# A new order at both ends of a fused attention and gated-convolution kernel, and a broadcast split over two DMA queues

## The chip, the cores and the metric

The kernel runs on one core of one Trainium2 chip. The metric is the device time of one execution in microseconds, and the comparison is between the median before the change and the median after it. The three runs of the kernel before took 1071.4, 1070.09 and 1071.84 us.

## The reference

Four independent batches. `q` has 12288 rows of 128 numbers per batch, `kv` is an image of 384 x 32 positions of 128 channels.

```python
kv_pool = kv.reshape(B, H // 4, 4, W // 4, 4, C).mean(axis=(2, 4))
k = v = kv_pool.reshape(B, -1, C) @ w_sr            # 768 keys per batch
s = (q @ k.T) / sqrt(C)
a = exp(s - s.max(-1)); a /= a.sum(-1) + 1e-9
x = a @ v                                            # attention output
gate_pre[t] = sum over k in 0..4 of conv_w[k] * x[t + k - 4]   # causal, zeros before the start
out = (sigmoid(gate_pre) * (x @ w_val)) @ w_out
```

The kernel works on transposed arrays, with the 128 channels as partitions and the rows of `q` along the free dimension.

## The kernel before

**Groups and tiles.** The rows of `q` are cut into 96 groups of 512 (24 for each batch), and a group into 4 tiles of 128 rows, `j` = 0 to 3. The main loop has one step for each tile, 384 in all. The order of the instructions on every engine is the order in which the Python code emits them (a manual schedule); each engine and each DMA queue works through its own list in that order. In the step of tile `j` of group `cur`, earlier groups are at later stages: `last` is one group behind, `avg` two, `xg` three, `mg` four, `og` five.

**One tile.** TensorE computes the scores (`score`, L264: each factor is split in a high and a low part, so three matmuls for each half of the 768 keys). VectorE takes the row maximum (`row_max`, L269, tile `nm`). ScalarE computes the exponentials and their sums (`expo`, L281). ScalarE writes the high part of the exponentials in 16 bits (`p_hi`, L328) and VectorE the low part (`p_lo`, L332, one step later). The exponentials must be transposed before the product with the values. This is done in one of two ways. For tiles `j < by_dma`, high and low parts go to `hl`, and SyncE's queue (SP) issues a DMA transpose from `hl` to `pt` (L336), one for tiles 0 and 1 and one for the rest. For the other tiles (`on_pe`) the exponentials go to `pf`, TensorE transposes them (`turn`, L311), and the parts are written straight to `pt`. Then TensorE multiplies with the values in 18 matmuls for each group (`av_range`, L345).

**The normaliser.** The four columns of sums of a group lie in `z`. When the group is complete, VectorE takes the reciprocal (L288) and transposes it to `r` (L293). `norm_store` (L299) writes the 512 numbers to a DRAM tile `rd` in four small DMAs, and `norm_rows` (L304) reads them back as one row that is broadcast to 128 partitions, into `rb`. In the loop both are on SP's queue: `norm_store(last)` at `j` = 1, `norm_rows(last)` at `j` = 3. `g_x` (L362) multiplies the product with `rb` and gives `x` of the group, one group after `norm_rows` was emitted.

**After x.** POOL computes the products of the convolution's taps (L372, the last tap on ScalarE, L370) and adds them (L381). ScalarE takes a tanh (`th`, L407), TensorE the value projection (`g_val`, L411), VectorE the gate (`g_h`, L416), TensorE the output projection (`g_out`, L421), ScalarE the scaled copy to `o` (`g_evac`, L431), and SP stores two groups together (L435). `new_x` copies the last 4 columns of the previous group's `x` ahead of the new one (L358). PSUM has three two-bank tiles for the scores (`bank_pair`, pool `ps_s`), one bank for `av` and one for all small products (`misc`, tile `m`).

**The start.** The first batch's `kv` comes in 16 pieces (tiles `kvt`, 384 KB each). Pieces 0, 2, 4 and 6 are pooled on POOL (L133), the others on VectorE (L121). When pieces 0 to 7 are pooled, and again after piece 13 and after piece 15, TensorE projects the finished keys (L146, tile `m`), ScalarE writes their high part (`kh`, L153) and the values (`vt`, L154), and VectorE the low part (`kl`, L157). The scores of the first three tiles follow: the first halves after the first projection, the second halves after the last.

**The end.** After the loop stands code written out by hand for the last five groups, `n1` (the last) to `n5`: the product of `n2`, the normaliser of `n1` (its `rd` and `rb` on ScalarE's queue), the product of `n1` in two halves of 256 rows (`avs`), then the convolutions of `n2` and `n1`, which `conv_mixed` splits between ScalarE (products in `kvt` tiles, L389) and VectorE (`fast`, L395, L397 and L401), and the projections and stores (L439).

Of the kernel before, what the change touches and what calls it, by code (L numbers as in the profile page):

```python
# [16 lines left out]
P = 128  # L17
GQ = 512
BLOCK = 32
NT = GQ // P  # L20


# [5 lines left out]
def attn_moe_kernel(ctx, tc, qT, kvT, w_sr, w_moe, outT):  # L28
# [34 lines left out]
    def misc():  # L63
        return ps_m.tile([P, GQ], F32, name="m")
# [185 lines left out]
    def bank_pair():  # L250
        return ps_s.tile([P, 2, GQ], F32, name="s")
# [42 lines left out]

    def norm_store(g, eng):

        g.rd = dram.tile([NT, P], F32, name="rd")
        for i in range(0, P, BLOCK):
            eng.dma_start(out=g.rd[:, i:i + BLOCK], in_=g.r[i:i + NT])  # L299

    def norm_rows(g, eng):
        g.rb = work.tile([C, GQ], F32, name="rb", bufs=3)
        row = g.rd.rearrange("(o j) p -> o (j p)", o=1)
        eng.dma_start(out=g.rb, in_=row.broadcast_to([C, GQ]))  # L304

    def turn(g, j):

# [3 lines left out]
            nc.tensor.transpose(g.s[j][:, k // (NCH // 2), c:c + P], pf[:, k * P:(k + 1) * P],  # L311
                                ident)

    def pt_tile(g):
        if g.pt is None:
            g.pt = ptp.tile([P, NT, 2 * NCH, P], F16, name="pt")
        return g.pt

    def part(g, j, a):

        if on_pe(g, j):
            return pt_tile(g)[:, j, a * NCH:(a + 1) * NCH].rearrange("p (h k) q -> p h (k q)", h=2)
# [7 lines left out]
    def p_lo(g, j):  # L330

        nc.vector.scalar_tensor_tensor(out=part(g, j, 1), in0=g.s.pop(j), scalar=2.0 ** 15,  # L332
                                       in1=part(g, j, 0), op0=ALU.mult, op1=ALU.subtract)
        if (j % 2 or j == g.by_dma - 1) and not on_pe(g, j):
            j0 = j // 2 * 2
            nc.sync.dma_start_transpose(  # L336
                out=pt_tile(g)[:, j0:j + 1].rearrange("p j k q -> p (j k) q"),
                in_=g.hl[:, j0:j + 1].rearrange("p j a k -> p (j a k)"))

    AV_ORDER = [(v, k, a) for k in range(NCH) for v, a in (("vh", 0), ("vl", 0), ("vh", 1))]  # L340
# [1 line left out]
    def av_range(g, out, lo, hi, j0=0, j1=NT):  # L342
        for i in range(lo, hi):
            v, k, a = AV_ORDER[i]
            nc.tensor.matmul(out, g.st[v][:, k * P:(k + 1) * P], g.pt[:, j0:j1, a * NCH + k],  # L345
                             start=(i == 0), stop=(i == len(AV_ORDER) - 1))

    def av_part(g, part):
# [94 lines left out]
    for b in range(B):  # L443
        for i in range(NG):
            g = Group()
            g.i, g.b, g.t0, g.st = len(groups), b, i * GQ, states[b]
            g.by_dma = 4 if i % 2 == 0 and (b == B - 1 or not 0 < i <= PIECES + 1) else 3
            g.s, g.nm, g.pf, g.hl, g.pt = {}, {}, {}, None, None
            groups.append(g)
    G = len(groups)  # L450

    def at(i):
# [17 lines left out]
    for i in range(1, PIECES + 1):  # L470
        if i - 1 + AHEAD < PIECES:
            load_kv(0, st, i - 1 + AHEAD)
        (pool_halving if i - 1 in by_pool else pool_kv)(st, i - 1)
        if low and i - 1 in ends:
            low()
        if i == PIECES // 2:
            g_qh(at(0))
            g_ql(at(0))
        if i in ends:
            project(st, ends[i], misc())  # L480
            high, low = split_keys(st, ends[i])
            high()
        if i == PIECES // 2 + 1:
            for j in first:
                score(at(0), j, (0,))
    low()
# [105 lines left out]
    gate2 = conv_mixed(n2, 0, GQ)  # L592
    n2.th = g_tanh(gate2)
    m2, o2 = pair_of(GQ)
    g_val(n2, m2)
    new_x(n1, n2, nc.scalar.copy)
    g_x(n1, avs[0], *cuts[0])
    h4 = g_h(n4.th, n4.m)
    n4.m = g_out(h4, misc())
    out_tile(n4)  # L600
    gates = [conv_mixed(n1, *cuts[0])]
    g_evac(n4, n4.m)
    store(n4)
    g_x(n1, avs[1], *cuts[1])
    m3, o3 = pair_of(GQ)
    g_val(n3, m3)
    g_out(g_h(n2.th, m2), o2)
    n3.th = g_tanh(n3.gate)
    ms = pair_of(half)
    g_val(n1, ms[0], *cuts[0])  # L610
    gates.append(conv_mixed(n1, *cuts[1]))
    out_tile(n2)
    g_evac(n2, o2)
    store(n2)
    g_out(g_h(n3.th, m3), o3)
    g_val(n1, ms[1], *cuts[1])
    n1.th = work.tile([C, GQ], F32, name="th")
    ths = [g_tanh(gate, n1.th[:, c0:c1]) for gate, (c0, c1) in zip(gates, cuts)]
    g_evac(n3, o3)
    store(n3)  # L620
    for th, m, o, c in zip(ths, ms, pair_of(half), cuts):
        g_evac(n1, g_out(g_h(th, m), o), *c)
        store(n1, *c)


# [26 lines left out]
```

## Time and profile before

| what | us |
|---|---|
| median of 3 runs | 1071.4 (1070.09 to 1071.84) |
| the profiled execution's own time | 1068.99 |
| its span (first to last instruction of the core) | 1067.2 |
| TensorE matmul busy in the span | 1021.7 (96%) |
| VectorE, ScalarE, POOL busy | 918.1 (86%), 910.6 (85%), 874.5 (82%) |

The span is what the views of the profile show, from 0 to 1067.2 us; the execution's own time is 1.8 us longer. PE means TensorE's matmuls, PEld its weight loads, DVE VectorE, ACT ScalarE, SPq and ACTq the DMA-issuing instructions on SyncE's and ScalarE's queues. In a row of the timeline stand the start, the duration, the engine, the line, the operation, output and input, the count, and in brackets how long the engine stood idle before it and what ended that. A row of the chain (the work that ended last, followed back) has a start, a length and a piece of work. In a table by stretches stand, for each engine, the busy time and the count, then the granted clock of TensorE, the busy share of the 16 DMA engines, and GB/s.

### The profile page before, as it was taken

To read this page: it belongs to the slowest core of one execution; us is meant where nothing else is said; L and a number is where in the kernel's file an instruction comes from. 1 tells how busy PE (TensorE), PEld (TensorE's weight loads), DVE (VectorE), ACT (ScalarE), POOL (GpSimd) and SP (SyncE) were. 2 spreads that over 40 slices of the span, in tenths; PEclk is the share of its full clock that TensorE was granted. 3 is DMA by queue.
4 is the path that set the end of the run, shared out by engine and by line. 5 is a ranking of instruction groups with operands and counts; after the bars stand their busy time and mean duration, and the time that the engine had idled before them with its cause. 6 is when DMAs were issued, how large, how long until landed. Compare 5 with 4: busy or idle time off the path is not lost.

```text
span 1067.2 us, 16368 instructions
## 1 busy us (share of the span) xinstructions
PE 1021.7 (96%) x4912; PEld 686.6 (64%) x4912; DVE 918.1 (86%) x1283; ACT 910.6 (85%) x1671; POOL 874.5 (82%) x964
## 2 busy tenths in 40 slices
PE   2799999999999999999999999999999999999996
PEld 1666666666666666666666666666666666666663
DVE  6788899898888999999888999999888888888885
ACT  1788888888988888889888888888898898988883
POOL 4178888888888888888888888888888898988882
PEclk9999999999999999999999999999999999999999
DMA  8699999999999999999999999999999899989984
GB/s 288 120 219 218 221 216 241 216 201 208 199 209 231 218 242 223 223 216 212 195 199 231 238 225 217 245 213 200 196 210 207 198 208 215 207 192 200 211 178 123
DMA packets 526263, 224.96 MB, mean 211 GB/s; under 512 B 492640, under 2 KB 493024, under 8 KB 526176
## 3 DMA queue, kind: packets, MB, share of 16 engines
q1 hardware_dynamic: 526000, 223.66, 97.4%
q8 instruction: 39, 0.64, 0.2%
q14 instruction: 48, 0.39, 0.1%
q10 hardware_dynamic: 176, 0.26, 0.1%
HBM read 75.83 MB, written 25.36 MB: 95 GB/s over the span
## 4 chain that ended last, share of the span: by engine, by line
PE 74%; DVE 11%; ACT 9%; POOL 2%; issue 2%; DMA 2%; SPq 0%; DVEq 0%; ACTq 0%; POOLq 0%
PE s L264 30%; PE av L345 25%; PE m L411 7%; PE m L421 5%; PE s L311 4%; ACT s L281 4%; DVE nm L269 3%; ACT hl L328 2%; DVE h L416 2%; POOL ql L248 2%; DVE x L362 1%; DVE hl L332 1%; ACT qh L244 1%; DMA rb<-rd 1%; PE m L146 1%
## 5 line engine op out<-in xcount | busy, mean ns | idle before, releaser
L345 PE MATMUL av<-pt,vh 128*128 128x512 f16 x1140 | 386.9, 381 | 1.8 <-DVE x L362 1.4
L381 POOL TENSOR_TENSOR sum<-sum,tap 128x512 f32<-128x512 f32 x282 | 361.1, 1280 | 22.1
L269 DVE TENSOR_REDUCE nm<-s 128x1 f32<-128x768 f32 x384 | 361.4, 941 | 2.0 <-PE s L264 1.9
L281 ACT ACTIVATE s<-s,nm 128x768 f32<-128x768 f32 x312 | 272.5, 873 | 76.9 <-DVE nm L269 73.3
L372 POOL TENSOR_SCALAR tap<-x,wm 128x512 f32<-128x512 f32 x376 | 253.4, 693 | 80.0 <-DVE x L362 78.5
L332 DVE SCALAR_TENSOR_TENSOR hl<-s,hl 128x768 f16<-128x768 f32 x312 | 296.9, 952 | 23.8 <-ACT hl L328 23.6
L264 PE MATMUL s<-kh,qh 128*128 128x384 f32 x768 | 257.0, 415 | 8.1 <-DVE pw L174 2.1
L328 ACT ACTIVATE hl<-s 128x768 f16<-128x768 f32 x312 | 252.6, 810 | 9.1
L345 PEld LDWEIGHTS <-vh 128*128 128x128 f16 x1164 | 113.5, 97 | 178.4 <-issue 79.7
L345 PE MATMUL av<-pt,vl 128*128 128x512 f16 x570 | 216.0, 379 | 0.0
L264 PE MATMUL s<-kl,qh 128*128 128x384 f32 x768 | 198.8, 339 | 0.3 <-DVE kl L157 0.3
L264 PE MATMUL s<-kh,ql 128*128 128x384 f32 x768 | 198.8, 339 | 0.0
L264 PEld LDWEIGHTS s<-kh,qh 128*128 128x128 f32 x768 | 137.8, 191 | 65.8 <-issue 29.1
L248 POOL TENSOR_TENSOR ql<-q,qh 128x512 fp32r<-128x512 f32 x96 | 122.1, 1272 | 66.1 <-ACT qh L244 65.6
L264 PEld LDWEIGHTS s<-kl,qh 128*128 128x128 f32 x768 | 140.7, 190 | 0.8 <-DVE kl L157 0.7
L264 PEld LDWEIGHTS s<-kh,ql 128*128 128x128 f32 x768 | 140.5, 190 | 0.0
L381 POOL TENSOR_TENSOR sum<-tap,tap 128x512 f32<-128x512 f32 x94 | 119.8, 1274 | 0.0
L362 DVE SCALAR_TENSOR_TENSOR x<-av,down,rb 128x512 f32<-128x512 f32 x95 | 71.3, 751 | 46.8 <-POOL ql L248 28.7
L345 PEld LDWEIGHTS <-vl 128*128 128x128 f16 x582 | 57.1, 98 | 77.7 <-issue 54.5
L416 DVE SCALAR_TENSOR_TENSOR h<-th,m 128x512 f32<-128x512 f32 x93 | 64.0, 688 | 49.7 <-PE m L411 47.7
L411 PE MATMUL m<-x,wm 128*128 128x512 f32 x186 | 95.7, 596 | 0.0
L421 PE MATMUL m<-h,wm 128*128 128x512 f32 x186 | 94.9, 591 | 0.4 <-DVE h L416 0.4
(65 smaller groups left out, 918.2 us busy)
## 6 DMA issues: line engine op xcount, KB each, us to landing
kvt<-in_kv SPq DMA_DIRECT2D x64, 384.0 KB
rb<-rd SPq DMA_DIRECT2D x95, 256.0 KB
q<-in_q SPq DMA_DIRECT2D x47, 512.0 KB
out<-o SPq DMA_DIRECT2D x46, 512.0 KB
rd<-r SPq DMA_DIRECT2D x380, 0.5 KB
pt<-hl SPq DMA_TRANSPOSE x192
out<-o SPq DMA_DIRECT2D x3, 256.0 KB
q<-in_q SPq DMA_DIRECT2D x2, 256.0 KB
```

The lines of the kernel that those rows point to most:

```text
L248: nc.gpsimd.tensor_tensor(out=g.ql, in0=g.q, in1=g.qh.bitcast(F32), op=ALU.subtract)
L264: nc.tensor.matmul(g.s[j][:, h], a[:, sl], k[:, h * HALF:(h + 1) * HALF], start=(i == 0), stop=(i == 2))
L269: nc.vector.tensor_reduce(out=nm, in_=g.s[j], axis=AX.XY, op=ALU.max, negate=True)
L281: nc.scalar.activation(out=halves(g.pf[j]) if on_pe(g, j) else g.s[j], in_=g.s[j], func=AF.Exp, bias=g.nm.pop(j), accum_out=g.z[:, j:j + 1])
L328: nc.scalar.activation(out=part(g, j, 0), in_=g.s[j], func=AF.Copy, scale=2.0 ** 15)
L332: nc.vector.scalar_tensor_tensor(out=part(g, j, 1), in0=g.s.pop(j), scalar=2.0 ** 15, in1=part(g, j, 0), op0=ALU.mult, op1=ALU.subtract)
L345: nc.tensor.matmul(out, g.st[v][:, k * P:(k + 1) * P], g.pt[:, j0:j1, a * NCH + k], start=(i == 0), stop=(i == len(AV_ORDER) - 1))
L372: eng.tensor_scalar(out=g.tap[k], in0=src, scalar1=w, scalar2=1.0, op0=ALU.mult, op1=ALU.mult)
L381: nc.gpsimd.tensor_tensor(out=s, in0=acc, in1=g.tap[k], op=ALU.add)
L411: nc.tensor.matmul(m, wval, g.x[:, HALO + c0:HALO + c1], start=True, stop=True)
L416: nc.vector.scalar_tensor_tensor(out=h, in0=th, scalar=1.0, in1=m, op0=ALU.add, op1=ALU.mult)
L421: nc.tensor.matmul(m, wout, h, start=True, stop=True)
```

## The change

It has four parts.

1. `norm_store` writes the reciprocals twice (`rd` has two copies), and `norm_rows` reads them in two DMAs: the even partitions of `rb` from the first copy on the queue that it used before, the odd partitions from the second copy on ScalarE's queue. This holds for all 96 groups.
2. At the start, VectorE's low part of the first keys is emitted one piece later, and that of keys 384 to 671 after the last piece instead of before it.
3. In the last group two tiles instead of one go over TensorE (`by_dma` is 2 instead of 3), into a `pt` tile of their own, so that the product of its second half does not touch the DMA transpose's tile.
4. The hand-written end has another order. The halves of `n1`'s product are computed in the order (second, first) and, like most small products of the end, lie in two-bank tiles of their own. The copy ahead of `n2`'s `x` is emitted before ScalarE's `rb` DMAs. `h` of `n4` comes ahead of the convolution of `n2`, and both halves of `n1`'s `x` ahead of its convolution.

```diff
     def norm_store(g, eng):
-        g.rd = dram.tile([NT, P], F32, name="rd")
+        g.rd = dram.tile([COPIES, NT, P], F32, name="rd")
         for i in range(0, P, BLOCK):
-            eng.dma_start(out=g.rd[:, i:i + BLOCK], in_=g.r[i:i + NT])
+            part = g.r[i:i + NT]
+            eng.dma_start(out=g.rd[:, :, i:i + BLOCK].rearrange("k j c -> j k c"),
+                          in_=part.rearrange("j (o c) -> j o c", o=1).broadcast_to(
+                              [NT, COPIES, BLOCK]))
     def norm_rows(g, eng):
         g.rb = work.tile([C, GQ], F32, name="rb", bufs=3)
-        row = g.rd.rearrange("(o j) p -> o (j p)", o=1)
-        eng.dma_start(out=g.rb, in_=row.broadcast_to([C, GQ]))
+        rows = g.rd.rearrange("k j p -> k (j p)")
+        for k, q in enumerate((eng, nc.scalar)):
+            q.dma_start(out=g.rb[k:C:COPIES], in_=rows[k:k + 1].broadcast_to([C // COPIES, GQ]))
...
+    def pt_tile(g, j):
+        k = g is groups[-1] and on_pe(g, j)
+        if k not in g.pt:
+            g.pt[k] = ptp.tile([P, NT, 2 * NCH, P], F16, name="pt")
+        return g.pt[k]
...
+    groups[-1].by_dma = 2
...
-        if low and i - 1 in ends:
+        if low and i == PIECES // 2 + 2:
             low()
+            low = None
...
         if i in ends:
+            if low:
+                low()
             project(st, ends[i], misc())
...
-    def pair_of(width):
-        both = bank_pair()
-        return both[:, 0, :width], both[:, 1, :width]
+    def bank(width=GQ):
+        return bank_pair()[:, 0, :width]
...
     g_conv(n3)
+    new_x(n2, n3, nc.scalar.copy)
     p_lo(n1, NT - 1)
     store_pair(n5)
     norm_rows(n1, nc.scalar)
-    avs = pair_of(half)
-    av_range(n1, avs[0], 0, len(AV_ORDER), 0, NT // 2)
     n4.m = g_val(n4, misc())
-    av_range(n1, avs[1], 0, len(AV_ORDER), NT // 2, NT)
-    new_x(n2, n3, nc.scalar.copy)
+    avs = [bank(half) for _ in cuts]
+    for i in (1, 0):
+        av_range(n1, avs[i], 0, len(AV_ORDER), i * NT // 2, (i + 1) * NT // 2)
     g_x(n2, n2.av)
+    h4 = g_h(n4.th, n4.m)
+    n4.m = g_out(h4, misc())
     gate2 = conv_mixed(n2, 0, GQ)
+    n2.m = g_val(n2, bank())
...
+    g_evac(n4, n4.m)
+    n2.th = g_tanh(gate2)
+    new_x(n1, n2, nc.scalar.copy)
+    g_x(n1, avs[1], *cuts[1])
+    g_x(n1, avs[0], *cuts[0])
...
```

**The start on VectorE.** From the first pooled piece of VectorE on, before:

```order
L121 TENSOR_REDUCE pool<-kvt 128x48 x5
L157 SCALAR_TENSOR_TENSOR kl<-m,kh 128x384
L121 TENSOR_REDUCE pool<-kvt 128x48 x6
L157 SCALAR_TENSOR_TENSOR kl<-m,kh 128x288
L121 TENSOR_REDUCE pool<-kvt 128x48
L157 SCALAR_TENSOR_TENSOR kl<-m,kh 128x96
```

And after the change (its lines are numbered one higher at this place):

```order
L122 TENSOR_REDUCE pool<-kvt 128x48 x6
L158 SCALAR_TENSOR_TENSOR kl<-m,kh 128x384
L122 TENSOR_REDUCE pool<-kvt 128x48 x6
L158 SCALAR_TENSOR_TENSOR kl<-m,kh 128x288
L158 SCALAR_TENSOR_TENSOR kl<-m,kh 128x96
```

One pooled piece has moved ahead of the first low part and another ahead of the second.

**The last group and the end on ScalarE.** From the third tile of the last group on, before (`s` and `hl` are the way by DMA, `pf` and `pt` that over TensorE):

```order
L281 ACTIVATE s,z_103<-s,nm 128x2x384
L328 ACTIVATE hl<-s 128x768
L281 ACTIVATE pf,z_103<-s,nm 128x768
L285 ACTIVATE z_103<-z_103 128x4
L431 ACTIVATE o<-m 128x512
L328 ACTIVATE pt<-s 128x768
L299 DMA rd<-r 4x32 x4
L407 ACTIVATE th<-sum_12126 128x512
L370 ACTIVATE tap_12202<-x,wm 128x512
L304 DMA rb<-rd 128x512
L358 COPY x<-x 128x4
L389 ACTIVATE kvt<-x,wm 128x512 x2
```

And after:

```order
L282 ACTIVATE pf,z_103<-s,nm 128x768
L335 ACTIVATE pt<-s 128x768
L309 DMA rb<-rd 64x512
L282 ACTIVATE pf,z_103<-s,nm 128x768
L286 ACTIVATE z_103<-z_103 128x4
L438 ACTIVATE o<-m 128x512
L335 ACTIVATE pt<-s 128x768
L301 DMA rd<-r 4x2x32 x4
L414 ACTIVATE th<-sum_12220 128x512
L377 ACTIVATE tap_12304<-x,wm 128x512
L365 COPY x<-x 128x4
L309 DMA rb<-rd 64x512 x2
```

A DMA of `rb` now stands between the third tile's `pt` and the fourth tile's exponentials, and the copy stands ahead of the last `rb` DMAs. In every earlier group the same row, `DMA rb<-rd 64x512`, stands behind the fourth tile's `hl` or `pt` and ahead of the next group's first exponentials.

**The end on VectorE.** From the `x` of `n2` on, before:

```order
L362 SCALAR_TENSOR_TENSOR x<-av,down,rb 128x512
L395 TENSOR_SCALAR fast<-x,wm 128x512
L397 SCALAR_TENSOR_TENSOR fast<-x,wm,fast 128x512 x2
L401 TENSOR_TENSOR fast<-fast,kvt 128x512 x2
L362 SCALAR_TENSOR_TENSOR x<-s,down,rb 128x256
L416 SCALAR_TENSOR_TENSOR h<-th,m 128x512
L395 TENSOR_SCALAR fast<-x,wm 128x256
L397 SCALAR_TENSOR_TENSOR fast<-x,wm,fast 128x256 x2
L401 TENSOR_TENSOR fast<-fast,kvt 128x256 x2
L362 SCALAR_TENSOR_TENSOR x<-s,down,rb 128x256
L416 SCALAR_TENSOR_TENSOR h<-th,s 128x512
```

And after:

```order
L369 SCALAR_TENSOR_TENSOR x<-av,down,rb 128x512
L423 SCALAR_TENSOR_TENSOR h<-th,m 128x512
L402 TENSOR_SCALAR fast<-x,wm 128x512
L404 SCALAR_TENSOR_TENSOR fast<-x,wm,fast 128x512 x2
L408 TENSOR_TENSOR fast<-fast,kvt 128x512 x2
L369 SCALAR_TENSOR_TENSOR x<-s,down,rb 128x256 x2
L402 TENSOR_SCALAR fast<-x,wm 128x256
L404 SCALAR_TENSOR_TENSOR fast<-x,wm,fast 128x256 x2
L408 TENSOR_TENSOR fast<-fast,kvt 128x256 x2
L423 SCALAR_TENSOR_TENSOR h<-th,s 128x512
```

`h` of `n4` has moved ahead of the convolution of `n2`, and the second half of `n1`'s `x` ahead of the first half's convolution. On ScalarE, `o` of `n4` now stands ahead of the tanh of `n2`, and `o` of `n2` ahead of the products for `n1`'s second half.

More of the change, by code (lines that the diff above doesn't have):

```diff
@@ L19 @@
 BLOCK = 32
+COPIES = 2
 NT = GQ // P
@@ L312, in turn @@
                                 ident)
[L314 to L317, printed above, removed]
+    def pt_tile(g, j):
[3 more added lines that the diff above has]
+        return g.pt[k]
     def part(g, j, a):
         if on_pe(g, j):
-            return pt_tile(g)[:, j, a * NCH:(a + 1) * NCH].rearrange("p (h k) q -> p h (k q)", h=2)
+            return pt_tile(g, j)[:, j, a * NCH:(a + 1) * NCH].rearrange("p (h k) q -> p h (k q)", h=2)
         if g.hl is None:
@@ L336, in p_lo @@
             nc.sync.dma_start_transpose(
-                out=pt_tile(g)[:, j0:j + 1].rearrange("p j k q -> p (j k) q"),
+                out=pt_tile(g, j)[:, j0:j + 1].rearrange("p j k q -> p (j k) q"),
                 in_=g.hl[:, j0:j + 1].rearrange("p j a k -> p (j a k)"))
@@ L447, in attn_moe_kernel @@
             g.by_dma = 4 if i % 2 == 0 and (b == B - 1 or not 0 < i <= PIECES + 1) else 3
[L448 removed]
+            g.s, g.nm, g.pf, g.hl, g.pt = {}, {}, {}, None, {}
             groups.append(g)
+    groups[-1].by_dma = 2
     G = len(groups)
@@ L482, in attn_moe_kernel @@
             high()
-        if i == PIECES // 2 + 1:
+        if i == PIECES // 2 + 2:
             for j in first:
@@ L585, in attn_moe_kernel @@
     norm_rows(n1, nc.scalar)
-    avs = pair_of(half)
-    av_range(n1, avs[0], 0, len(AV_ORDER), 0, NT // 2)
     n4.m = g_val(n4, misc())
-    av_range(n1, avs[1], 0, len(AV_ORDER), NT // 2, NT)
-    new_x(n2, n3, nc.scalar.copy)
+    avs = [bank(half) for _ in cuts]
+    for i in (1, 0):
+        av_range(n1, avs[i], 0, len(AV_ORDER), i * NT // 2, (i + 1) * NT // 2)
     g_x(n2, n2.av)
[L592 to L597, printed above, removed]
     h4 = g_h(n4.th, n4.m)
     n4.m = g_out(h4, misc())
+    gate2 = conv_mixed(n2, 0, GQ)
+    n2.m = g_val(n2, bank())
     out_tile(n4)
-    gates = [conv_mixed(n1, *cuts[0])]
     g_evac(n4, n4.m)
     store(n4)
+    n2.th = g_tanh(gate2)
+    new_x(n1, n2, nc.scalar.copy)
     g_x(n1, avs[1], *cuts[1])
-    m3, o3 = pair_of(GQ)
-    g_val(n3, m3)
-    g_out(g_h(n2.th, m2), o2)
-    n3.th = g_tanh(n3.gate)
-    ms = pair_of(half)
-    g_val(n1, ms[0], *cuts[0])
-    gates.append(conv_mixed(n1, *cuts[1]))
[L612 to L622, printed above, removed]
+    g_x(n1, avs[0], *cuts[0])
+    n3.m = g_val(n3, misc())
+    gates = [conv_mixed(n1, *cuts[0])]
+    h2 = g_h(n2.th, n2.m)
+    m1s = [g_val(n1, bank(half), *cuts[0])]
+    n2.m = g_out(h2, bank())
+    n3.th = g_tanh(n3.gate)
+    m1s.append(g_val(n1, bank(half), *cuts[1]))
+    out_tile(n2)
+    g_evac(n2, n2.m)
+    store(n2)
+    ths = [g_tanh(gates[0], work.tile([C, GQ], F32, name="th")[:, :half])]
+    gates.append(conv_mixed(n1, *cuts[1]))
+    h3 = g_h(n3.th, n3.m)
+    n3.m = g_out(h3, misc())
+    ths.append(g_tanh(gates[1], work.tile([C, GQ], F32, name="th")[:, :half]))
+    for i, (th, m, c) in enumerate(zip(ths, m1s, cuts)):
+        o = g_out(g_h(th, m), bank(half))
+        if i == 0:
+            g_evac(n3, n3.m)
+            store(n3)
+        g_evac(n1, o, *c)
         store(n1, *c)
```

2 lines of the change are left out of this document (1 added, 1 removed).

## The prediction

> **What bounds the kernel now.** I read the page's busy table first, then the table by stretches, then the chain of work that ended last in the middle, at the start and at the end, and last the waits and the timeline at the places that the change touches.
>
> ```profile
> PE 1021.7 (96%) x4912; PEld 686.6 (64%) x4912; DVE 918.1 (86%) x1283; ACT 910.6 (85%) x1671; POOL 874.5 (82%) x964
> ...
> PE 74%; DVE 11%; ACT 9%; POOL 2%; issue 2%; DMA 2%; SPq 0%; DVEq 0%; ACTq 0%; POOLq 0%
> ```
>
> TensorE carries three quarters of the chain. The next rows say where it does not, and how full the DMA engines are:
>
> ```profile
> core 0: us, PE busy (x) PEld busy (x) DVE busy (x) ACT busy (x) POOL busy (x), PEclk, DMA share, GB/s
> 0.00:40.00 40.00, 15.05 (x40) 10.95 (x41) 27.97 (x46) 12.90 (x24) 13.75 (x25) 1.00 0.68 224
> 120.00:340.00 220.00, 218.25 (x1067) 147.68 (x1066) 194.79 (x272) 196.24 (x360) 190.02 (x209) 1.00 1.01 216
> 1040.00:1067.00 27.00, 17.71 (x74) 8.78 (x71) 13.57 (x24) 9.71 (x20) 7.76 (x8) 0.94 0.45 121
> ```
>
> In the loop (third row) TensorE is busy 218.25 of 220 us, and the DMA engines hold a packet all the time (share 1.01). TensorE idles for 25 us of the first 40 and 9 us of the last 27. The chain between 400 and 440 us is TensorE alone:
>
> ```profile
> by line: PE s L264 41.0%; PE av L345 35.9%; PE m L411 8.6%; PE m L421 8.6%; PE s L311 6.6%
> ```
>
> So the loop can gain only where TensorE waits there, and both ends are chains of dependent work, in which an order decides.
>
> **Part 1: the start.** The chain, with VectorE's pooling in it:
>
> ```profile
> 18.49 0.56 DVE kl L157
> 19.05 4.31 DVE pool L121 x5
> ...
> 23.40 1.34 PE m L146 x2
> ...
> 24.76 0.41 ACT kh L153
> 25.17 0.31 ACT vt L154
> ...
> 25.51 0.46 DVE kl L157
> 25.97 0.87 DVE pool L121
> ...
> 26.88 0.75 PE m L146 x2
> ```
>
> Five pieces are pooled between the first `kl` and the second projection; after the change four. VectorE's timeline shows where the fifth goes:
>
> ```profile
> 14.88 1.96 DVE L121 TENSOR_REDUCE pool<-kvt 128x48 f32<-128x768 f32 x2 [1.58 <-DMA kvt<-in_kv]
> 18.49 0.56 DVE L157 SCALAR_TENSOR_TENSOR kl<-m,kh 128x384 fp32r<-128x384 f32 x1 [1.66 <-ACT vt L154]
> ```
>
> Before 18.49 VectorE stood idle for 1.66 us, and a piece takes 0.87, so the moved piece is hidden there if its `kvt` has landed. That is an estimate: the first of these pieces ended the wait at 14.86, and a 384 KB piece at the 224 GB/s of the first row is 1.75 us, at twice that rate 0.9, so the third lands between 16.7 and 18.4. At the late end `kl` slips by 0.8 and the gain of this part is gone. Back-to-back pooling of later pieces in the row of the chain (0.86 us each, no wait) says the early end is nearer. Then the second projection starts 0.7 earlier (a piece of 0.87, less 0.17 for its landing, my estimate), at 22.7. The last piece now stands ahead of the second `kl`, where VectorE would wait for `vt`. That `kl` keeps its distance of 25.97 - 23.40 = 2.57 us from the projection and ends at 25.27. The last projection shares tile `m` with it, so it follows there and not at 26.88: **-1.6 us**. Bounds: 0 (data late) and -1.7 (the piece moved plus the 0.87 of the last one).
>
> **Part 2: the loop.** VectorE's `x` sometimes waits for the broadcast. The waits over the whole span, the longest case in the chain, and the loop's places where ScalarE has slack:
>
> ```profile
> DVE x L362 <- DMA rb<-rd: 5.1, 5, 1.7
> ```
>
> ```profile
> 106.46 4.58 DMA rb<-rd
> ...
> 111.18 0.16 DVE x L362
> ```
>
> ```profile
> 137.88 2.00 SPq L299 DMA_DIRECT2D rd<-r  x4
> 138.59 0.88 ACT L281 ACTIVATE s<-s,nm 128x768 f32<-128x768 f32 x1 [0.45 <-DVE nm L269]
> 142.86 0.81 ACT L328 ACTIVATE pt<-s 128x768 f16<-128x768 f32 x1 [0.32 <-PE s L311]
> 143.93 0.88 ACT L281 ACTIVATE s<-s,nm 128x768 f32<-128x768 f32 x1 [0.25 <-DVE nm L269]
> ```
>
> What can be gained: 5.1 us in 5 waits. SP's half is 128 KB, which at 216 GB/s is 0.6 us less to move: at most 5 x 0.6 = 3.0 us of VectorE's waits. TensorE does not feel all of that. I take **-1.5** (bounds 0 and -5.1).
>
> The Trainium skill ("DMA: Bandwidth & Descriptors", Rules for kernel authors) advises against two transfers to disjoint partition halves, since both share the same engines and serialise. The share of 1.01 agrees that no engine is free for a second queue; by that rule the -1.5 is 0 and the total 1.5 us later. Whether reading the row from two copies is quicker, no row here shows.
>
> What it costs: ScalarE issues 95 more DMAs in the loop, each of which waits for the four `rd` DMAs; behind it on ScalarE stands the next group's first exponential (143.93). How long an `rd` takes to land is bounded by the two places where the issue of `rb` visibly waited for it:
>
> ```profile
> 1036.95 1.43 SPq L299 DMA_DIRECT2D rd<-r  x4
> ...
> 1039.64 0.35 SPq L304 DMA_DIRECT2D rb<-rd  x1
> ...
> 1039.81 0.81 ACT L328 ACTIVATE pt<-s 128x768 f16<-128x768 f32 x1 [0.24 <-PE s L311]
> ...
> 1039.98 1.68 ACTq L299 DMA_DIRECT2D rd<-r  x4
> ...
> 1045.76 0.36 ACTq L304 DMA_DIRECT2D rb<-rd  x1
> ```
>
> That is 1.26 us (1038.38 to 1039.64) to 4.10 us (1041.66 to 1045.76) after the issue. ScalarE's `rd` issue ran from 1039.98 while its own `pt` ran until 1040.62, so a DMA without a wait hides behind the activation ahead of it. In the group at 137.88 the `rd` are issued by 139.88 and land between 141.14 and 143.98; `pt` ends at 143.67. At the late end the exponential starts at 143.98 + 0.36 = 144.34 instead of 143.93, 0.41 late. The idle 0.45 at the same engine two tiles on (138.59, the group before) takes that up before TensorE's transposes need `pf`. So most groups cost nothing; where the cover is used up, the delay shifts ScalarE once and the next `rd` is then early enough. I put one shift of 0.41 in about two stretches: **+0.8** (0 to +9.5, the upper end if 0.1 us leaked in each of 95 groups). Writing `rd` twice adds 512 bytes and no DMA; SP's issues stay as many, its cost is put at 0, hidden behind SP's transposes. The low price is nearest to the rows, since DMA rows of SP are not on the chain (SPq 0%).
>
> **Part 3: the end.** The tail's chain and idle rows:
>
> ```profile
> 1036.13 1.00 ACT s L281 x2
> ...
> 1038.90 0.87 PE s L311 x6
> ...
> 1052.63 0.48 DVE x L362
> ...
> 1059.43 0.61 DVE h L416
> ...
> 1060.09 1.13 PE s L421 x2
> ...
> 1064.14 0.38 ACT o L431
> ```
>
> ```profile
> 1043.82 0.75 DVE L362 SCALAR_TENSOR_TENSOR x<-av,down,rb 128x512 f32<-128x512 f32 x1 [2.21 <-PE av L345]
> 1046.38 0.49 DVE L395 TENSOR_SCALAR fast<-x,wm 128x512 f32<-128x512 f32 x1 [1.81 <-ACT x L358]
> 1052.63 0.48 DVE L362 SCALAR_TENSOR_TENSOR x<-s,down,rb 128x256 f32<-128x256 f32 x1 [1.71 <-PE s L345]
> 1058.28 0.60 ACT L431 ACTIVATE o<-s 128x512 f32<-128x512 f32 x1 [0.87 <-PE s L421]
> 1063.40 0.30 PEld L421 LDWEIGHTS s<-h,wm 128*128 128x128 f32 x2 [0.88 <-ACT o L431]
> ```
>
> *Later.* The third tile now goes over TensorE: exponential until 1037.13, transposes 0.87, `pt` 0.81, so 1038.9. Behind it on ScalarE stands the new `rb` DMA, which waits for the same `rd` as SP's at 1039.64, and issues in 0.36. The fourth exponential starts at 1040.0; before, it followed the third and an `hl` of 0.81 at 1037.9. All behind it, `x` of `n2` included, comes **2.1 later** (`x` at 1045.9). *Earlier.* The 1.81 of idle time behind it goes, since the copy is no longer behind the `rd` wait, but `h` of `n4` (0.69 for an `h`) comes in: the convolution of `n2` starts at 1045.9 + 0.75 + 0.69 = 1047.3 instead of 1046.38. It ended at 1050.93 (1052.63 - 1.71), so now at 1051.9. The idle 1.71, in which `x` of `n1` waited for both halves in one tile, goes as well: `x` at 1051.9 instead of 1052.63, and both halves are done by 1052.8. What lay between `x` and the last `h` before (6.8 us from 1052.63 to 1059.43) now lacks one `h` (0.68), but `o` of `n4` and the tanh of `n2` stand ahead of the copy on ScalarE (+0.8), and `o` of `n2`, with its projection of 1.13, ahead of the last products (+1.2; both are estimates, from an `o` of 0.60 and that projection, less what VectorE does meanwhile). So the last big `h` starts at 1051.9 + 6.8 - 0.7 + 0.8 + 1.2 = 1060.0 instead of 1059.43. *Behind it.* Before, `n1`'s second projection waited 0.88 for ScalarE's `o` because both lay in one tile, and a small projection stood between; from that `h` to the last `o` took 4.7 us. Now the three projections follow each other: `h` 0.6, 1.13, then on ScalarE `o` 0.60, 0.38 and 0.38 = 3.1. The last `o` is at about 1063.1 less its own 0.38, 1062.7 instead of 1064.14: **-1.4 us**. I take -1.2 for waits between them. Bounds: -3.3 if the `rd` wait of 2.1 is not there, +0.8 if the new places on ScalarE cost twice the 2.0 that I gave them.
>
> **The sum.** -1.6 - 1.5 + 0.8 - 1.2 = -3.5 us. On the profiled execution's own 1068.99 that is 1065.5. That execution lies 2.4 us below the median of the runs shown; carried to the median 1071.4 the forecast is **1067.9 us**.
>
> **The rivals.** *The broadcast gains in full:* all 5.1 us of waits go and ScalarE is never late: -1.6 - 5.1 - 1.2 = -7.9, 1063.5. For it, the waits are on the chain (4.58 us at 106.46); against it, full DMA engines and a TensorE with only 1.75 idle us in 220. *ScalarE waits (slower):* `rd` sits behind long transfers on SP's queue, lands later than the 4.10 in most groups, and the exponential behind the new DMA is late by more than the idle 0.45. It decides from (2.8 + 2.1) / 95 = 0.05 us of leak in each group; at 0.08 the loop costs +7.6 without a gain, 1071.4 + 7.6 - 2.8 = 1076.2. For it: a 2.00 us issue ending only 3.8 us ahead of `pt`'s end. Against it: the shift helps the next group. *The halves serialise:* no gain in the loop and the +0.8 remains: 1071.4 - 2.8 + 0.8 = 1069.4. The rule of the Trainium skill above would give this one. *The end gives nothing:* the late fourth exponential eats what the order gives: -1.6 - 1.5 + 0.8 = -2.3, 1069.1, or nothing at all where the start's data are late.
>
> **How the numbers follow.** Forecast 0.38 (own range 1066 to 1069.2), full gain 0.14, halves serialise 0.20, the end gives nothing 0.14, ScalarE waits 0.14. A measurement tells a change from none at about 0.2%, here 2.1 us: faster is below 1069.3, slower above 1073.5. Faster takes the forecast and the full gain, 0.52; same the serialised halves and the dead end, 0.34; slower ScalarE's wait, 0.14. The range reaches into the full gain on one side and towards ScalarE's wait on the other: 1064.5 to 1073.2.
>
> **What would show it.** Start: the last projection of the keys at about 25.3 instead of 26.88. Loop: the row of `x` waiting for `rb` below 5.1; a new row of ScalarE's exponential, or of its queue, waiting for `rd`, short and few; TensorE busy as in 120 to 340. End: the fourth exponential of the last group some 2 us later against the first than before, the idle 1.81 and 1.71 gone, and less than 4.7 us from the last large `h` to the last `o`. The forecast is wrong if ScalarE waits for `rd` in most groups and TensorE's transposes wait for `pf` behind it, or if `kl` at the start waits for a `kvt`.

## The result, and the profile after

The changed kernel takes 1063.43 us (median of four runs, 1062.75 to 1065.12) against 1070.86 for the kernel before (1070.09 to 1071.84): -7.4 us, ratio 0.9937, 95% interval 0.9914 to 0.9959. Forecast were 1067.9 and -3.5; the range began at 1064.5. The profiled execution took 1063.95 us, 5.0 less than the profiled one of before, which is the fastest seen of the kernel before in its session. Later sessions gave medians of 1063.60 to 1064.54 for the changed kernel and 1068.92 to 1073.71 for the one before: the new median is steady, the old one is not. Single executions of the changed kernel reached from 1062.11 to 1068.21.

The first page and the table by stretches of the changed kernel:

```profile
PE 1021.1 (96%) x4918; PEld 687.7 (65%) x4918; DVE 919.2 (87%) x1283; ACT 911.7 (86%) x1671; POOL 876.0 (82%) x964
...
0.00:40.00 40.00, 17.25 (x48) 13.14 (x49) 29.21 (x50) 15.00 (x28) 13.84 (x25) 0.98 0.72 232
120.00:340.00 220.00, 218.29 (x1064) 147.65 (x1063) 195.14 (x272) 197.16 (x360) 191.34 (x208) 1.00 1.02 213
1035.00:1062.00 27.00, 18.77 (x80) 10.05 (x80) 15.48 (x28) 10.73 (x24) 7.83 (x8) 0.87 0.36 107
```

TensorE's work is the same but for the six transposes of one more tile (4918 matmuls instead of 4912), and it does 2.2 us more of it in the first 40 us. In 120 to 340 hardly anything differs, busy time or DMA share: the profiled execution of before was already undisturbed there, and none of its five waits for `rb` lies in that stretch. In the last stretch the mean granted clock is 0.87, where before had 0.94.

The start, from the chain of work:

```profile
18.57 3.45 DVE pool L122 x4
...
22.07 1.34 PE m L147 x2
...
24.17 0.47 DVE kl L158
...
24.69 0.75 PE m L147 x2
```

Four pieces instead of five stand between the first `kl` and the second projection, and the last projection starts at 24.69, 2.2 us earlier than before. Some 0.5 of that is data that came earlier: the wait for the first `kvt` ends at 14.40 instead of 14.88.

What was new in the waits, and the row to which it points:

```profile
ACT s L282 <- DVE r L294: 3.3, 2, 1.9
```

```profile
343.51 0.46 ACTq L309 DMA_DIRECT2D rb<-rd  x1
344.02 0.88 ACT L282 ACTIVATE s<-s,nm 128x768 f32<-128x768 f32 x1 [1.90 <-DVE r L294]
```

ScalarE waits twice, 1.9 us at the longest, in its new `rb` DMA. The row of `x` waiting for `rb` (5.1 us before) is gone. In the two profiled executions, the stretch from the first group's sums (`z`, on ScalarE) to those of the last group but one, the loop without both ends, shortened from 991.0 to 988.5 us.

### The profile page after: what moved, and what is told of

The parts are those of the page before. It is cut to its first block, busy times and chain, and to the rows that moved or that the text cites. A ratio compares the mean times of both kernels' runs of the same rounds, so it can differ in the third digit from the quotient of the medians.

```text
span 1062.2 us, 16578 instructions
## 1 busy us (share of the span) xinstructions
PE 1021.1 (96%) x4918; PEld 687.7 (65%) x4918; DVE 919.2 (87%) x1283; ACT 911.7 (86%) x1671; POOL 876.0 (82%) x964
## 4 chain that ended last, share of the span: by engine, by line
PE 75%; DVE 11%; ACT 8%; POOL 2%; DMA 1%; issue 1%; ACTq 0%; SPq 0%; DVEq 0%
PE s L265 31%; PE av L352 26%; PE m L418 7%; PE m L428 6%; PE s L316 4%; DVE nm L270 4%; ACT s L282 4%; ACT hl L335 2%; POOL ql L249 2%; DVE hl L339 2%; DVE h L423 2%; DVE x L369 1%; ACT qh L245 1%; PE m L147 1%; DMA rd<-r 1%
```

## Experiments

The kernels of one table ran on one chip beside the kernel before; times are compared inside a table only.

### The three parts alone

The first edit takes only the hunks of the start, the second only `norm_store` and `norm_rows`, the third only `pt_tile`, `by_dma = 2` and the hand-written end.

> The kernel before with the new order at the start alone (VectorE's two low parts of the keys one piece later, the scores of the first halves one piece later). Forecast's term: -1.6 us. Rival, that the data are late: 0. If the order alone counts and not the earlier data of that one execution: the last projection of the keys 1.7 us earlier against the start of the kvt wait, and -1.7 in the time, since the loop after it is bound by TensorE.

> The kernel before with the two copies of 1/z and the broadcast in two DMAs over two queues alone; both ends as before (in the last group the odd half of the broadcast stands on ScalarE's queue). Forecast's terms: -1.5 + 0.8 = -0.7 us. 'The broadcast gains in full': -5.1. 'The halves serialise' (the rule of the Trainium skill, DMA: Bandwidth & Descriptors, Rules for kernel authors): +0.8. From the two profiles, in which the loop of the changed kernel gained about 2.5 us: -2.5. The row of VectorE's x waiting for rb disappears in the first, second and fourth case; a row of ScalarE's exponential waiting for VectorE's r (through rd) appears, some 2 to 3 us.

> The kernel before with the last group's two tiles over TensorE and the new order of the end alone; the broadcast is one DMA on one queue, so no DMA stands ahead of the last group's fourth exponential. Forecast's bound without that wait of 2.1 us: -3.3. 'The end gives nothing': 0. From the two profiles (the end took 0.4 us less with a wait of 1.2 us ahead of the fourth exponential): -1.6.

> The changed kernel once more, beside its three parts. If the parts add up and the difference of the profiled executions is the true one: -5.0 us; if the difference of the medians is: -7.4. The parts by the forecast: -1.6 - 0.7 - 1.2 = -3.5.

| kernel | median us (runs, range) | ratio to before (95%) |
|---|---|---|
| before | 1073.71 (23, 1070.80 to 1079.92) | |
| start alone | 1073.29 (12, 1069.59 to 1077.90) | 0.9983 (0.9964 to 1.0001) |
| broadcast alone | 1064.22 (6, 1063.80 to 1065.74) | 0.9894 (0.9875 to 0.9913) |
| end alone | 1074.56 (12, 1072.70 to 1078.90) | 1.0002 (0.9987 to 1.0017) |
| whole change | 1064.54 (6, 1062.89 to 1066.92) | 0.9894 (0.9874 to 0.9915) |

The broadcast alone makes the whole gain here, nearly twice what its highest expectation said, and with it the scatter shrinks from 9 to 2 us (4 in the whole change). The waits of VectorE's `x` in the two kernels that keep the old broadcast say why, first the start alone, then the end alone:

```profile
DVE x L362 <- DMA rb<-rd: 18.7, 18, 1.8
```

```profile
DVE x L365 <- DMA rb<-rd: 13.4, 14, 1.6
```

The execution on which the prediction rests had 5 such waits, these have 18 and 14. They are the same instructions on the same data. The loop's length follows the waits: from the first group's sums to those of the last group but one it took 991.0 us with 5.1 us of them (before), 996.2 with 13.4 (end alone), 1000.0 with 18.7 (start alone), and 987.7 with none (broadcast alone). So by these four executions each us of waits costs some 0.6 to 0.7 us, an estimate.

### What of the broadcast counts

```diff
# one_copy: two queues, but both DMAs read one copy
+        for k, q in enumerate((eng, nc.scalar)):
+            q.dma_start(out=g.rb[k:C:2], in_=row.broadcast_to([C // 2, GQ]))
# one_queue: two copies, both DMAs on SP
-        for k, q in enumerate((eng, nc.scalar)):
+        for k, q in enumerate((eng, eng)):
# halves: partitions 0-63 and 64-127 instead of even and odd
-            q.dma_start(out=g.rb[k:C:COPIES], ...
+            q.dma_start(out=g.rb[k * (C // COPIES):(k + 1) * (C // COPIES)], ...
# whole_on_act: the kernel before, whole broadcast from ScalarE's queue
-            norm_rows(last, nc.sync)
+            norm_rows(last, nc.scalar)
```

> The kernel before with the broadcast in two DMAs (even partitions on SP's queue, odd ones on ScalarE's) that both read the one copy of 1/z. If the second queue makes the gain: as the split with two copies, about 9 us below before (0.990 to 0.993), no row of x waiting for rb. If the second copy makes it (fewer reads of one row): close to before (1.000), 13 to 19 us of x waiting for rb.

> The kernel before with two copies of 1/z and two DMAs by partition parity, both on SP's queue. If the second queue makes the gain: as before (1.000) or slower by one more issue on SP, x waits for rb as before. If the two copies make it: about 9 us below before.

> As the split alone (two copies, two queues), but the first DMA fills partitions 0 to 63 and the second 64 to 127 instead of the even and the odd ones. If parity doesn't matter: about 9 us below before, as the split by parity. If the rule of the Trainium skill on disjoint partition halves (DMA: Bandwidth & Descriptors, Rules for kernel authors) holds here for halves but not for parity: the two serialise, and the time is near before (1.000).

> The kernel before with the whole broadcast as one DMA from one copy on ScalarE's queue in the loop; nothing is split. If what counts is that the broadcast leaves SP's queue: about 9 us below before or more, no row of x waiting for rb, ScalarE waits for rd as in the split (2 to 5 us). If the split itself counts (each half is 0.6 us less to move): x still waits for rb, and the time lies between, 3 to 6 us below before.

| kernel | median us (runs, range) | ratio to before (95%) |
|---|---|---|
| before | 1068.92 (17, 1066.72 to 1075.74) | |
| one_copy | 1063.84 (6, 1063.75 to 1064.91) | 0.9950 (0.9930 to 0.9970) |
| one_queue | 1092.90 (6, 1089.97 to 1098.37) | 1.0221 (1.0191 to 1.0251) |
| halves | 1067.18 (12, 1064.26 to 1070.67) | 0.9978 (0.9962 to 0.9994) |
| whole_on_act | 1063.03 (6, 1062.88 to 1064.29) | 0.9943 (0.9923 to 0.9962) |

The gain needs neither the second copy nor the split: one copy is enough (one_copy), and one unsplit DMA on ScalarE's queue gains as much. The same split on SP's queue alone costs 24 us. So what SP's queue has to work through decides. SP's timeline in the kernel before, in a usual group, and below it the timeline of VectorE with `r` and `x` of that group:

```profile
204.31 7.70 SPq L336 DMA_TRANSPOSE pt<-hl  x2
212.19 0.80 SPq L304 DMA_DIRECT2D rb<-rd  x1
213.04 1.33 SPq L299 DMA_DIRECT2D rd<-r  x4
214.48 5.30 SPq L336 DMA_TRANSPOSE pt<-hl  x2
219.96 0.79 SPq L304 DMA_DIRECT2D rb<-rd  x1
```

```profile
208.08 0.21 DVE L293 STREAM_TRANSPOSE r<-z 128x32 f32<-128x32 f32 x1
...
226.62 0.75 DVE L362 SCALAR_TENSOR_TENSOR x<-av,down,rb 128x512 f32<-128x512 f32 x1
```

SP issues nearly without a gap, and most of its time goes into the two transposes. `r` is ready at 208.29, but SP is still in the two transposes ahead, and issues the four `rd` only at 213.04. Then the next two transposes stand ahead of `rb`, which goes out at 219.96. By the trace's landing of each DMA the last `rd` had landed at 216.35 and `rb` landed at 224.77, 1.85 us ahead of `x`. Between 120 and 860 us SP spends 666 of 740 us issuing (464 of them in 141 transposes, 3.3 us each; 52 in 70 broadcasts). The changed kernel, SP, ScalarE's queue and VectorE:

```profile
207.12 1.52 SPq L301 DMA_DIRECT2D rd<-r  x4
209.74 5.29 SPq L343 DMA_TRANSPOSE pt<-hl  x2
215.20 0.75 SPq L309 DMA_DIRECT2D rb<-rd  x1
```

```profile
213.34 0.48 ACTq L309 DMA_DIRECT2D rb<-rd  x1
```

```profile
204.72 0.21 DVE L294 STREAM_TRANSPOSE r<-z 128x32 f32<-128x32 f32 x1
...
223.07 0.75 DVE L369 SCALAR_TENSOR_TENSOR x<-av,down,rb 128x512 f32<-128x512 f32 x1
```

ScalarE's half goes out 8.4 us after `r`. SP's half still stands behind the transposes, at 10.3, but has half the bytes and lands at 219.10, 4.0 us ahead of `x`. The same times over the groups, worked out from the start and the landing of every DMA in the trace (us from the end of `r`, medians; `groups` is how many of the 95 groups are in it, and all 95 together give values within 0.5 us of these; the last column is how far `rb` landed ahead of the start of `x` in the tenth of the groups where that was least):

```
kernel          groups  rd landed  last rb issued  rb landed  x starts   rb ahead of x, 10%
before            92       8.17        11.77         16.56      18.14        0.13
start alone       90       8.84        12.66         17.23      18.32        0.13
changed kernel    93       6.71        11.14         14.38      18.14        2.26
one_copy          93       6.57        10.94         14.39      18.14        2.32
halves            92       6.74        11.30         14.77      18.14        1.73
whole_on_act      93       6.05         8.39         12.72      18.14        4.09
one_queue         73       9.28        14.34         17.29      18.50        0.13
```

In the kernel before the broadcast is issued 3.6 us after its data have landed, and in a tenth of the groups `x` starts as soon as it lands: its margin is used up. The margin comes back in two ways. In whole_on_act the broadcast goes out sooner, 8.39 instead of 11.77 us after `r`. In the changed kernel SP's half keeps its place behind the transposes; it lands 1.8 us earlier than the whole broadcast did (means over 95 groups: 14.36 against 16.14 us after `r`), 0.8 of it because SP comes to it sooner and 1.0 because half the bytes land sooner after their issue (3.3 against 4.3). With one_queue each broadcast costs SP two issues, 89 us instead of 52 in the same stretch, and the whole queue falls behind:

```profile
DVE x L367 <- DMA rb<-rd: 29.0, 22, 3.3
...
PEld L350 <- DMA pt<-hl: 9.2, 4, 5.2
```

Now the transposes are late too, and TensorE waits for `pt`. In halves one `x` waits (1.4 us), and ScalarE waits more than in the changed kernel:

```profile
ACT s L282 <- DVE r L294: 7.4, 4, 2.4
...
ACT s L282 <- DVE z L289: 4.0, 3, 1.4
```

Contiguous halves are 3.3 us slower than parity with one copy on the same chip, and each lands 0.3 us later after its issue (3.53 and 4.32 us against 3.21 and 4.04, medians). But the two kernels differ in the number of copies as well, and in the broadcast alone, by parity with two copies, ScalarE's half also takes 4.41 us to land. So why halves are slower stays open. The rule of the Trainium skill that the prediction weighed ("DMA: Bandwidth & Descriptors", Rules for kernel authors) is to use one transfer, as two to disjoint partition halves serialise. The runs agree in so far as one DMA is as fast as the split by parity (1063.03 against 1063.84), and differ in that the halves still gain a little over before (0.9962 to 0.9994); how parity would differ it does not say.

### The start and the end on a steady base

On the kernel before, 9 us of scatter hide a term of 1.7. With the broadcast split they can be read. `split_start` is the split and the start; the whole change adds the end; `warm` adds idle work for TensorE to the end:

```diff
-    m1s = [g_val(n1, bank(half), *cuts[0])]
+    pairs = [bank_pair()]
+    m1s = [g_val(n1, pairs[0][:, 0, :half], *cuts[0])]
+    for _ in range(2):
+        g_val(n2, pairs[0][:, 1])          # result not used
...
-    m1s.append(g_val(n1, bank(half), *cuts[1]))   # and the same two behind this one
```

> The split of the broadcast alone once more, as the base of the next three on the same chip: its runs scatter by 2 us, those of the kernel before by 9 us, so what the start and the end are worth can be read on this base. Expected 1064 us whatever before takes.

> The split and the new start, with the old end. If the start's 1.7 us reach the end: 1.7 below split_again. If ScalarE's waits for rd or the rest of the pipeline eat part of it, as the profile of the whole change beside that of the split suggests (1.70 at the first group's sums, 0.7 to 0.9 left at the last): 0.8 below.

> The whole change, beside split_start: the difference of the two is the end alone. By the forecast's term: 1.2 us below split_start. By the profiles (from the sums of the last group but one to the end of the span 36.6 to 38.5 us with the old end, 38.1 to 38.2 with the new): 0 to 1.5 us above it.

> The whole change with two idle value projections (results not used) in each of the two gaps of TensorE in the end, ahead of the output projections of n2 and of n3. In the whole change's profile TensorE idles 2.46 and 2.12 us there, its granted clock falls to 0.60 and 0.50, and n3's output projection takes 2.07 us instead of 1.13. If the clock falls because of the gaps and costs the end its gain: those projections at 1.13 again and 1.2 to 1.6 us below all_third. If the clock falls for another reason, or VectorE is the limit there: the same time.

| kernel | median us (6 runs each) | range |
|---|---|---|
| before (11 runs) | 1070.81 | 1067.42 to 1072.07 |
| split_again | 1065.03 | 1064.46 to 1066.40 |
| split_start | 1063.35 | 1062.41 to 1065.05 |
| whole change | 1063.60 | 1062.51 to 1065.58 |
| warm | 1063.34 | 1062.86 to 1065.37 |

The split is worth -5.8 here, the start -1.7, the end +0.25, which is nothing within the scatter. The ranges of split_again and split_start overlap a little, so the start's -1.7 is a difference of medians. The end's chain in the changed kernel:

```profile
1034.34 1.00 ACT pf L282 x2
...
1046.93 0.88 DVE x L369 x2
...
1050.36 0.61 DVE h L423
...
1054.66 0.61 DVE h L423
...
1055.31 2.07 PE m L428 x2
1057.38 1.61 PE s L428 x4
1059.02 0.38 ACT o L438
```

From the last large `h` (1054.66) to the start of the last `o` it takes 4.4 us, where 2.7 were forecast (3.1 to the end of that `o`) and before took 4.7. The largest part is the projection of `n3`, which needs 2.07 us instead of 1.13. TensorE's rows and the stretches:

```profile
1051.02 1.32 PE L428 MATMUL s<-h,wm 128*128 128x512 f32 x2 [2.46 <-DVE h L423]
...
1055.31 2.07 PE L428 MATMUL m<-h,wm 128*128 128x512 f32 x2 [2.12 <-DVE h L423]
```

```profile
1047.00:1051.00 4.00, 1.31 (x4) 0.30 (x2) 3.61 (x10) 2.15 (x5) 0.00 (x0) 1.00 0.17 66
1051.00:1055.00 4.00, 2.17 (x4) 0.82 (x4) 2.39 (x6) 1.70 (x4) 0.00 (x0) 0.60 0.17 66
1055.00:1058.00 3.00, 2.69 (x4) 1.20 (x5) 1.01 (x3) 1.00 (x2) 0.00 (x0) 0.50 0.00 0
```

The new order collects the value projections early, so TensorE idles 2.46 and 2.12 us later, and its granted clock falls to 0.60 and 0.50 just there. With the idle projections in the gaps (warm, the first two views), and in the old end with the split (the broadcast alone, the last two), the matching stretches keep the full clock:

```profile
1051.00:1055.00 4.00, 3.26 (x9) 1.44 (x8) 2.58 (x7) 1.70 (x4) 0.00 (x0) 1.00 0.13 52
1055.00:1058.00 3.00, 2.02 (x7) 0.97 (x6) 1.63 (x4) 1.29 (x3) 0.00 (x0) 1.00 0.05 18
```

```profile
1055.93 1.14 PE m L428 x2
```

```profile
1055.80 1.13 PE L426 MATMUL s<-h,wm 128*128 128x512 f32 x2 [1.41 <-DVE h L421]
```

```profile
1052.00:1056.00 4.00, 1.76 (x5) 0.88 (x6) 3.46 (x8) 2.23 (x5) 0.00 (x0) 1.00 0.30 118
```

The longest gap in the broadcast alone from 1047 us on is 1.41 us; one of 1.80 us ahead of 1037.27 left the clock at 1.00 as well. All five profiles with the new end and empty gaps have the low clock there, and the three with the gaps filled do not. So the nearly idle stretch around these gaps causes it, and in the profiled executions the stretch from the last group's sums (`z`) to the last `o` shortens from 23.5 to 22.0 us, inside the expected 1.2 to 1.6. The medians show 0.3, less than their scatter: what 1.5 us at the end are worth in the median isn't settled by these six runs.

What the end is worth depends on the broadcast. From the sums of the last group but one to the last `o` the old end takes 35.5 us in the kernel before, but 34.1 to 34.4 in the broadcast alone, split_again and split_start. The new end takes 35.0 to 35.1 in the whole change (35.8 in its slowest profile). With the idle projections it takes 33.6. So behind the split the new order is 0.7 to 1.0 us longer in most profiles, and shorter than the old one once the clock is kept up.

### The place in SP's queue, and a combined version

`early` keeps one DMA and one queue, and moves the broadcast ahead of one transpose; `moved` leaves it where it was and takes the loads of `q` and the stores of `out` off SP; the last two put the whole broadcast on ScalarE's queue, with the new start and the old end, or with the new end and the idle projections.

```diff
# early
+        if last and nxt and j == 3:
+            norm_rows(last, nc.sync)
         drip()
         if prev:
             p_lo(prev, (j - 1) % NT)
...
-        if last and nxt and j == 3:
-            norm_rows(last, nc.sync)
```

> The kernel before with its one broadcast DMA on SP's queue as it was, but one place earlier in that queue: ahead of the DMA transpose of the third tile instead of behind it. If the gain comes from when the broadcast is issued (in the kernel before it is issued 11.8 us after VectorE's r, median of 92 groups, though rd has landed after 8.2; a transpose's issue takes 3.3 us): the issue moves to 8.5 to 9, no row of x waiting for rb, and the time is as the split's, 5 us below before. If a second queue is needed: 0. If SP now waits for rd and the transposes behind it are late: rows of TensorE's av waiting for pt, and slower than before.

> The kernel before with the broadcast untouched on SP's queue, but the loop's loads of q and stores of out issued from ScalarE's queue instead. That takes 27 us of issues off SP's 666 in the 740 us from 120 to 860. If SP's queue is late because it is nearly full: the broadcast is issued about 1 us earlier, x waits less for rb (below 5 us), 2 to 5 us below before, unless ScalarE stalls behind a load of q. If only the broadcast's own place counts: 0.

> The whole broadcast on ScalarE's queue in the loop (one copy, one DMA) and the new start, with the old end. If both add up (-1.7 for the start): 1061.4 us, 2 us below the whole change; if ScalarE's later place eats the start: 1063.

> As whole_start, with the new end and the idle projections in TensorE's gaps; no DMA on ScalarE stands ahead of the last group's fourth exponential. If the wait there (1.2 us) and the low clock (1.5 us) are what the new end lost: 1 to 1.5 us below whole_start, 1060.2 us. If the new end gives nothing even so: as whole_start.

| kernel | median us (runs, range) | ratio to before (95%) |
|---|---|---|
| before | 1072.46 (11, 1069.73 to 1079.86) | |
| early | 1065.99 (6, 1062.45 to 1068.35) | 0.9929 (0.9903 to 0.9955) |
| moved | 1085.99 (6, 1080.47 to 1088.55) | 1.0110 (1.0082 to 1.0138) |
| whole_start | 1062.37 (4, 1061.21 to 1063.77) | 0.9897 (0.9870 to 0.9924) |
| whole_start_warm | 1062.71 (4, 1062.21 to 1063.14) | 0.9901 (0.9871 to 0.9932) |

SP's timeline of `early`:

```profile
208.05 2.09 SPq L299 DMA_DIRECT2D rd<-r  x4
210.87 3.54 SPq L336 DMA_TRANSPOSE pt<-hl  x1
214.59 0.48 SPq L304 DMA_DIRECT2D rb<-rd  x1
215.16 1.61 SPq L336 DMA_TRANSPOSE pt<-hl  x1
```

One transpose stands between `rd` and `rb` instead of two (two stood there in the 72 of 96 groups with three tiles by DMA; with four it was one before as well). Over 93 groups the broadcast is issued at 9.75 (median, us from `r`) instead of 11.77 and lands at 13.51 instead of 16.56; no `x` waits for it, and the time falls by 6.5 us. No second queue, no split and no second copy is needed: that the broadcast goes out too late in SP's queue is the cause of the old loop's waits. Its runs scatter more (6 us) than those with the whole broadcast on ScalarE's queue (1 to 3).

`moved` is slower. Its waits, and ScalarE's timeline at the longest of the first:

```profile
ACT s L281 <- DMA pt<-hl: 12.9, 6, 3.5
...
DVE x L362 <- DMA rb<-rd: 8.1, 7, 2.0
```

```profile
141.13 0.34 ACTq L233 DMA_DIRECT2D q<-in_q  x1
141.57 0.88 ACT L281 ACTIVATE s<-s,nm 128x768 f32<-128x768 f32 x1 [3.50 <-DMA pt<-hl]
```

The exponential stands right behind a load of `q` in ScalarE's queue, and the load itself is issued late (by the profile until a `pt` transpose has landed; why is open). `x` still waits, 8.1 us in all.

The broadcast goes out 0.8 us earlier but lands no earlier (16.89), so whether a less full SP queue alone would help stays open.

The new end with the idle projections adds nothing to whole_start in time (1062.71 against 1062.37, where 1 to 1.5 us less were expected). The profiles agree: from the sums of the last group but one to the last `o` both take 33.5 to 33.6 us, so where ScalarE has no DMA of `rb` ahead of the fourth exponential, the old end is as short as the new one with the idle projections. The last two beat before as clearly as the whole change does. whole_start_warm ran once more beside the whole change, under the name `combined`:

> The whole change once more, beside the combined version on the same chip: 1063.5 us.

> The whole broadcast on ScalarE's queue, the new start, the new end and the idle projections, beside the whole change on the same chip. If the 1.5 us of TensorE's clock and the 1.2 us ahead of the fourth exponential add up: 1.5 to 2.5 us below the whole change, 1061 to 1062 us. If run-to-run scatter of 2 us hides that: within 0.1% of it.

The whole change took 1063.99 us (6 runs, 1062.11 to 1068.21; ratio to before 0.9916, 0.9896 to 0.9937), the combined version 1062.53 (4 runs, 1062.25 to 1063.33; 0.9907, 0.9885 to 0.9929). It is 1.5 us lower in the median and steadier, but the intervals overlap: not shown to be faster.

## Why the prediction was right or wrong

**The start: right.** -1.6 was forecast, -1.7 measured (split_start against split_again); alone on the old base it was -0.4, which the scatter there hides. The third piece's data were there at the early end, as taken. The last projection of the keys came at 24.69 where 25.3 was named, with data 0.5 us earlier.

**The loop's gain: the step that failed.** -1.5 with a bound of -5.1 was forecast; the split gave -5.8 on the steadiest comparison and -9.5 on another chip. The mechanism was there (`x` waits for the broadcast, and an earlier landing removes the wait), but both factors of "at most 5 x 0.6" were too small. First, the 0.6: "SP's half is 128 KB, which at 216 GB/s is 0.6 us less to move" takes the broadcast as late by its bytes alone. SP's half landed 1.8 us earlier, 1.0 of it from the bytes and 0.8 because SP's queue came to it sooner, a term that the prediction does not have. The old broadcast is late mainly by its place: 3.6 us pass between the landing of `rd` and the issue of `rb`, with two transposes in between in most groups, and early and whole_on_act remove the waits with all the bytes in one DMA. The rows of SP that show it stand in the same timeline as the row at 137.88 that the prediction used for ScalarE's cost. It took "SPq 0%" in the chain as a reason to price SP at nothing; the queue issues for 666 of 740 us, and in the chain that shows as the wait for what it issues (4.58 us of `rb` at 106.46). Second, the 5: the waits of `x` in one execution were taken as all there is to gain, though that execution was 2.4 us below the median of its kernel. In that pair of executions the loop gained 2.5 us, inside the bounds; but the two other profiles with the old broadcast have 14 and 18 waits, and loops 5 and 9 us longer. The forecast carried the 2.4 us over unchanged; by those rows they belong to what the change removes. That the timed runs of before had as many waits is not shown, since they have no profile.

**The loop's cost: about right in kind, small beside the rest.** +0.8 in two shifts was forecast; the profile has two waits, 3.3 us together (1.8 to 6.6 us in three more profiles of the changed kernel). What they cost in time was not measured alone. The rival "ScalarE waits" did not decide: whole_on_act has no such row and is as fast.

**The end: wrong, "The end gives nothing" holds.** -1.2 was forecast, +0.25 measured. The fourth exponential came later, as forecast, but by 1.2 us (between the sums of the two profiled executions) instead of 2.1. Nearly all of that is the third tile's way over TensorE: the issue of `rb` (1033.83 to 1034.29) ends 0.1 us after `pt`, so the wait for `rd`, 1.1 us of the forecast, was not there in this execution. The path from that exponential to the last large `h` came out nearly as forecast (20.0 us by its numbers, 20.3 measured). What failed is the step "the three projections follow each other: `h` 0.6, 1.13": the durations came from rows at full clock, and the new order makes the gaps that lower it. That term was 3.1 to the end of the last `o` and measured 4.7.

**The rivals.** "The broadcast gains in full" came out at the right time, 1063.5, by a sum that is not the real one (-1.6 - 5.1 - 1.2; measured -1.7 - 5.8 + 0.25). It had a chance of 0.14; against it the prediction held the full DMA engines and TensorE's 1.75 idle us in 120 to 340, a stretch in which that execution had no such wait. That its time fits is luck. "The halves serialise" is refuted for the kernel as changed: the split alone gains 5.8 and 9.5 us, and in its profile no `x` waits. The Trainium skill's "DMA: Bandwidth & Descriptors" (section "Issuing engines are not separate DMA queues") states that issuing from several engines saves only the issuing time, usually small beside the DMA. The trace agrees with the first half: on ScalarE's queue the broadcast takes no less from issue to landing (4.40 against 4.11 us, medians). For the broadcast itself it agrees with the second as well (0.74 us to issue), but not for the transposes ahead of it (3.3 us to issue on the mean, 5.7 to the landing at the median), and their issuing is what the broadcast waits for.

## What to carry to other kernels

Read the queue that issues the DMAs as an engine: sum its issue times, and for a late transfer look first at what stands between the landing of its source and its own issue; a place one instruction earlier, or another queue, was worth 6 us here with the bytes unchanged. When the profiled execution is faster than every timed run, some wait may be short in it by chance; ask whether it is one that the change touches before carrying its time to the median. And when an order is rewritten, look at the gaps that it leaves on TensorE, not only at the sum of the steps.

## What the hardware showed that was not expected

- TensorE's granted clock averaged 0.60 in the four microseconds after a gap of 2.46 us and 0.50 in the three after, around another gap of 2.12, with 1.31 of 4 us busy in the stretch before. A projection of 128x512 took 2.07 us instead of 1.13 to 1.14.
- A gap's length alone does not tell: gaps of 2.23 us (early, ahead of 1042.58) and 2.73 us (moved, ahead of 144.87) left the clock at 1.00, one of 2.18 us in the kernel before (ahead of 1045.89) did not. In the clock records of the twenty profiles the clock changes between 1.00 and 0.50 only, and at distances that are multiples of 3.41 us. By these steps TensorE was busy 0.95 of 3.41 us ahead of the fall in the changed kernel and 1.25 ahead of that in the kernel before; it was busy 1.83 (early) and 1.57 (moved) where the clock held. Over all profiles it fell after steps with 44% or less busy (once 51%) and held after 46% and more, with busy times as the trace models them.
- One DMA issue more on SP for each of 95 groups cost 24 us (one_queue against before), 0.25 us a group, though SP's own share of the critical chain was 0%.
- The kernel whose two DMAs fill contiguous halves of the partitions was 3.3 us slower than one whose DMAs fill even and odd ones (1067.18 against 1063.84); the second reads one copy and the first two, so the cause is not settled.
